# A hand-made layout for the stage behind attention: weights first in the pool, x in fixed homes, x's low part made by VectorE, three homes for raw words

## The chip, the cores and the metric

The kernel runs on one core of one Trainium2 chip. The metric is the device time of one launch in microseconds (us), of which the median over several runs is given. A profile is one more execution, recorded by the hardware profiler. TensorE is called PE in the profile, VectorE DVE, ScalarE ACT, GpSimd POOL and SyncE, whose queue issues the DMAs here, SP or SPq.

## The reference

```python
scores = (q @ k.T) / sqrt(64)                     # 8 batches, 8 heads, 576 x 576
scores = where(scores >= rowmax - tau, scores, -1e9)
attn = softmax(scores)
x = (attn @ v), the heads side by side            # 4608 tokens x 512
h = x @ w_in                                      # 512 -> 2048, float64 weights
g = max(h, 0) + alpha * min(h, 0)
out = g @ w_out                                   # 2048 -> 512
```

## The kernel before, in words

TensorE multiplies numbers of a shortened fp32 form. For accuracy every operand is cut into a high part (rounded, "hi") and the rest ("lo"), and each product is made of three matmuls: hi by hi, hi by lo, lo by hi. The float64 weights come as raw 64-bit words. A chain of eight steps on ScalarE, VectorE and GpSimd, called decoding here, makes a hi and a lo tile of each. With 128 hidden rows to a slice there are 16 slices (`fc`), each with a tile of `w_in` and one of `w_out`.

The kernel has two stages.

1. Attention over 32 pairs of heads, with slices 0 to 6 of the second network worked in between for groups of 256 tokens. The finished x goes to DRAM (`xs`), the sum over the seven slices too (`part`).
2. The stage behind attention (`behind`, line 792). When the attention loop is through, its pool `ap1` is closed and a pool `wp2` is opened on the same bytes, with `reuse_waits="tile"`: each tile there waits for the earlier users of its own bytes. The stage finishes slices 0 to 6 for what is left of the tokens (jobs of kind a: a rest of the group at 3328, then the groups at 3584, 3840, 4096 and 4352), then does slices 7 to 10 for all tokens in nine jobs of 512 (kind b), then slices 11 to 15 (kind c). The last three groups of kind a need x of the last batch, which the last pair of heads completes.

A job has two kinds of steps. `step1` (line 853) is the first layer of one slice, called a unit: 12 matmuls (4 chunks of x by 3 terms), then on VectorE the two instructions of lines 859 and 860 that read the PSUM result and leave it in `pt`, then ScalarE's hi part of g (line 228) and GpSimd's lo part of g (line 231). `step2` (line 865) is the second layer of 128 tokens: 21 matmuls for kind a, 12 for b, 15 for c, and the way out of PSUM. There are four PSUM homes for units and four for second layers. The list `order` (line 910) puts the first unit of the next job ahead of the second-layer steps of the job at hand. Only where kind a meets kind b do the second-layer steps come first, so that the first job of kind b runs its four units in a row and the first unit of the next job straight behind them.

x comes in through `load` (line 839): one home `xr` for the raw x, two each for its hi part `xh` and its lo part `xl`. `load` of a job is called at the first step of the job before. The four chunks are then split one at the end of each step (`split`, line 847): ScalarE rounds the chunk into `xh` (line 850), and GpSimd subtracts (line 851). Chunks that are left when the job starts are split ahead of its first unit. The steps of decoding are also spread over the list (`starts`, line 924), each weight one step of the chain at a time: load (line 120), two conversions on ScalarE (lines 130 and 131), clamp and shift on VectorE (lines 134 and 137), sign and power (142 and 147), rounding on ScalarE (151), a product on GpSimd (825), a difference on VectorE (826) and a sum on GpSimd (165). The raw words of a weight have two homes (`w0`), its temporary three (`w1`).

PE, ACT, DVE and POOL issue their instructions in the order in which the code emits them (`manual_schedule`, line 956): each engine's queue is the order of the list above, and an instruction that waits holds everything behind it on its engine. The order on SP is set by the framework's scheduler.

The order of tags in `wp2` gives the addresses: `xr` comes first and lies over `qst0` and `qst1` (attention's scaled q), then `xh` and `xl` over `qst1` and the tiles `eo`, `e0` that attention's last product reads, then the raw words, the temporaries and the eight weight tiles.

Of the kernel before, what the change touches and what calls it, by code (L numbers as in the profile page):

```python
# [10 lines left out]
F32 = mybir.dt.float32  # L11
F32R = mybir.dt.float32r
I32 = mybir.dt.int32
U32 = mybir.dt.uint32
I64 = mybir.dt.int64
AF = mybir.ActivationFunctionType
ALU = mybir.AluOpType
# [4 lines left out]
P = 128  # L22
# [5 lines left out]
G2 = 512  # L28
# [7 lines left out]
GB = 11  # L36
ENG1 = ('vpp', 'vpp')
ENG2 = ('vvp', 'vvv')
# [25 lines left out]
def f(ap):  # L64
    return ap.bitcast(F32)
# [10 lines left out]
def tile_masked_attention_moe(  # L76
# [11 lines left out]
    nc = tc.nc  # L88
    B, NPAIR = q.shape[0], q.shape[1]
    NT, DM = out.shape  # L90
    NCC = DM // P
# [16 lines left out]
    class Split64:  # L108


        def __init__(self, pool, raw, temp_pool, temp, eng, src, a, name, split=False):
            self.split = split
            self.pool, self.raw_tag, self.temp_pool, self.temp_tag = pool, raw, temp_pool, temp
            self.eng = [nc.vector if e == 'v' else nc.gpsimd for e in eng]
            self.src, self.a, self.name = src, a, name

        def load(self):
            tag, bufs = self.raw_tag
            self.raw = self.pool.tile([P, DM], I64, tag=tag, name=f"wr{self.name}", bufs=bufs)
            nc.sync.dma_start(self.raw.rearrange("p (a b) -> p a b", a=self.a), self.src)  # L120

        def size(self):
            words = self.raw.bitcast(I32).rearrange("p (n two) -> p n two", two=2)
            self.low, self.high = words[:, :, 0], words[:, :, 1]
            tag, bufs = self.temp_tag
            pool = self.temp_pool
            if pool is mem:
                pool, tag, bufs = (mem.mp1, "g", GB) if mem.mp1 else (spool, "wt", 4)
            self.t = pool.tile([P, DM], I32, tag=tag, name=f"wt{self.name}", bufs=bufs)
            nc.scalar.activation(f(self.t), f(self.high), AF.Abs)  # L130
            nc.scalar.activation(f(self.low), self.low.bitcast(U32), AF.Copy, scale=2.0**-52)

# [40 lines left out]
    wi, wo = {}, {}  # L173
    ready = set()

    def weight(pool, fc, io):
        d = wi if io == "i" else wo
        d[fc] = pool.tile([P, 2, DM], F32R, tag=f"w{io}{fc}", name=f"w{io}{fc}")
        return d[fc]

    def load_x(pool, t0, n, gn, bufs):
        xr = pool.tile([P, NCC, gn], F32, tag=f"xr", name=f"xr{gn}_{t0}", bufs=bufs)
        t = t0
        while t < t0 + n:
            b, o = divmod(t, S)
            m = min(S - o, t0 + n - t)
            nc.sync.dma_start(xr[:, :, t - t0 : t - t0 + m], xs[b][:, :, o : o + m].rearrange("c p t -> p c t"))
            t += m
        return xr

    def split_x(pool, xr, t0, n, gn, bufs):
        xh = pool.tile([P, NCC, gn], F32R, tag="xh", name=f"xh{gn}_{t0}", bufs=bufs)
# [52 lines left out]
    spool = sp.enter_context(tc.tile_pool(name="spool", bufs=1, side="right"))  # L245
    mem = SimpleNamespace(mp1=None)
# [389 lines left out]
    for p in pairs:  # L636
        o = 9 * p.pi
        n = o - 9
# [138 lines left out]
    for n_, (w, fc, io) in enumerate(pieces):  # L777
        c = n_ * DEC_LAST // (len(pieces) - 1)
# [13 lines left out]
    def behind():  # L792
# [10 lines left out]
        wp2 = ctx.enter_context(tc.tile_pool(name="wp2", bufs=1, reuse_waits="tile"))  # L803
        ps_2 = ctx.enter_context(tc.tile_pool(name="ps_2", bufs=1, space=PSUM, reuse_waits="tile"))
        wpool = SimpleNamespace(b=None)
        part2 = [dram.tile([min(P, NT - t), DM], F32, name=f"part2{t}") for t in range(0, NT, P)]
        fa, fb = fcs2[:NA], fcs2[NA:]

        chores = deque()
        stages = deque()  # L810

        def decode(fc, io):
            w = Split64(wp2, ("w0", 2), wp2, ("w1", 3), ENG2[0], *(src_i if io == "i" else src_o)(fc))

            def put():
                w.round(weight(wp2 if fc in fa else wpool.b, fc, io)[:, 0])

            low, t = lambda: f(w.low), lambda: f(w.t)
            return [
                w.load,  # L820
                w.size,
                lambda: (w.clamp(), w.shift()),
                lambda: (w.sign(), w.power()),
                put,
                lambda: nc.gpsimd.tensor_tensor(low(), low(), f(w.high), op=ALU.mult),
                lambda: nc.vector.tensor_tensor(t(), t(), f(w.hi), op=ALU.subtract),
                lambda: w.join((wi if io == "i" else wo)[fc][:, 1]),
            ]

        class Job:  # L830
# [8 lines left out]
            def load(self):  # L839
                if self.x is not None:  # L840
                    return
                self.xr = load_x(wp2, self.t0, self.n, G2, 1)
                xh = wp2.tile([P, NCC, G2], F32R, tag="xh", name=f"xh{self.name}", bufs=2)
                xl = wp2.tile([P, NCC, G2], F32R, tag="xl", name=f"xl{self.name}", bufs=2)
                self.x = xh, xl

            def split(self, c):
                n = self.n
                xh, xl = self.x
                nc.scalar.activation(xh[:, c, :n], self.xr[:, c, :n], AF.Copy)  # L850
                nc.gpsimd.tensor_tensor(xl[:, c, :n], self.xr[:, c, :n], f(xh[:, c, :n]), op=ALU.subtract)

            def step1(self, i):
                fc, n, gn = self.fcs[i], self.n, self.gn
                pool, bufs = (mem.mp1, GB) if self.kind == "a" else (wpool.b, 2 * len(fb))
                name = f"{self.name}_{fc}"
                ph = layer1_into(ps_2.tile([P, 512], F32, tag="ph", name=f"ph{name}", bufs=4), fc, n, self.x)
                t = pool.tile([P, gn], F32, tag="pt", name=f"pt{name}", bufs=2)
                nc.vector.tensor_scalar(t[:, :n], ph[:, :n], 0.0, alpha_sb[:, fc : fc + 1], op0=ALU.min, op1=ALU.mult)
                nc.vector.scalar_tensor_tensor(t[:, :n], ph[:, :n], 0.0, t[:, :n], op0=ALU.max, op1=ALU.add)  # L860
                g = pool.tile([P, 2, gn], F32R, tag="g", name=f"g{name}", bufs=bufs)
                split_g(g, t, n)
                self.g[i] = g
# [42 lines left out]
        ja = [Job(fa, t, min(G2, NT - t), G2, "b") for t in range(0, NT, G2)]  # L906
        jb = [Job(fb, t, min(G2, NT - t), G2, "c") for t in range(0, NT, G2)]
        jobs = first + ja + jb

        order = []  # L910
        for a, b in zip([None] + jobs, jobs + [None]):
# [22 lines left out]
        for k, (job, what, i) in enumerate(order):  # L934
            if job.kind == "b" and wpool.b is None:
                p1.close()
                wpool.b = ctx.enter_context(tc.tile_pool(name="mp2", bufs=1, reuse_waits="tile"))
            for b in ahead.get(k, []):
                if b.x is None:
                    b.load()  # L940
                    xq.extend((b, c) for c in range(NCC))
            if what == 1:
                while xq and xq[0][0] is job:
                    b, c = xq.popleft()
                    b.split(c)
                job.step1(i)
            else:
                job.step2(i)
            for fn in starts.get(k, []):
                fn()  # L950
            if xq:
                b, c = xq.popleft()
                b.split(c)
# [110 lines left out]
```

## Time and profile before

| | us |
|---|---|
| median of 3 runs (1392.28 to 1394.5) | 1393.32 |
| the profiled execution, its own time | 1393.67 |
| its span, first to last instruction | 1391.7 |
| PE busy | 1338.2 |
| DVE busy | 993.8 |
| ACT busy | 842.4 |
| POOL busy | 834.1 |

The median lies 0.35 us under the time of the profiled execution. What lies around the span is 1393.67 - 1391.7 = 1.97 us. In the profile a row of a timeline gives the start in us from the beginning of the span, the duration, the engine, the line of the code, the operation, output and inputs, and the number of instructions that were put together in the row. In square brackets stands the idle time of the engine just before and the instruction that ended it. A row of the windows gives, for each engine, busy time and instructions in that stretch, then the clock that TensorE was granted, the busy share of the DMA engines, and GB/s. A row of the chain gives start, duration and the link of the chain of work that ended last.

### The profile page before, as it was taken

What the parts mean: (1) busy time and instruction counts of PE and PEld (TensorE: products, weight loads), DVE (VectorE), ACT (ScalarE), POOL (GpSimd) and SP (SyncE); (2) the same over time, 40 slices, a digit from 0 to 9 for tenths busy, and PEclk for the clock granted to TensorE, in tenths of its full rate; (3) what the DMA queues carried; (4) which work ended last, traced back from release to release, by engine and by line L of the source; (5) the groups of instructions that cost most, each with busy time, mean ns of one, the idle gap of its engine ahead of it and who ended that gap; (6) DMA issues with size and microseconds to landing.
All of it is one profiled execution on the core that took longest, in us unless ns stands there. A gap on an engine that the chain in (4) does not pass through costs nothing.

```text
span 1391.7 us, 23733 instructions
## 1 busy us (share of the span) xinstructions
PE 1338.2 (96%) x8116; PEld 1180.8 (85%) x8116; DVE 993.8 (71%) x1960; ACT 842.4 (61%) x1918; POOL 834.1 (60%) x963
## 2 busy tenths in 40 slices
PE   5888899999999999999999998999999999999998
PEld 4555789999999999999999997887888888888887
DVE  6999888889888888898898863762666644333332
ACT  7887888888888888888888862432323222211210
POOL 3887576576666666666576564774667564443431
PEclk9999999999999999999999999999999999999999
DMA  7653634644545445444454303334464543243222
GB/s 235 178 154 102 168 111 120 174 117 131 151 120 147 140 127 148 132 140 126 132 154 128 107 26 120 104 134 145 137 214 153 185 152 121 91 140 133 91 76 83
DMA packets 113448, 186.02 MB, mean 134 GB/s; under 512 B 16592, under 2 KB 47600, under 8 KB 113328
## 3 DMA queue, kind: packets, MB, share of 16 engines
q1 hardware_dynamic: 113328, 184.51, 44.5%
q8 instruction: 65, 1.06, 0.3%
q14 instruction: 55, 0.45, 0.1%
HBM read 104.41 MB, written 37.90 MB: 102 GB/s over the span
## 4 chain that ended last, share of the span: by engine, by line
PE 82%; DVE 6%; ACT 4%; POOL 3%; DMA 2%; issue 2%; SPq 1%; POOLq 0%; DVEq 0%; ACTq 0%
PE acca L237 11%; PE pha L207 11%; PE av L564 10%; PE s L417 10%; PE phc L207 9%; PE accc L237 9%; PE accb L237 7%; PE t L461 7%; PE phb L207 7%; DVE p L452 1%; DVE nmx L432 1%; PE tk L477 1%; DMA wri<-in_moe_w_in_dram 1%; POOL ga L231 1%; ACT xb L577 1%
## 5 line engine op out<-in xcount | busy, mean ns | idle before, releaser
L432 DVE TENSOR_REDUCE nmx<-s 128x1 f32<-128x576 f32 x288 | 217.2, 754 | 71.9 <-PE s L417 69.1
L237 PE MATMUL acca<-wo,ga 128*128 128x512 f32 x756 | 226.8, 417 | 2.5 <-POOL ga L231 0.8
L452 DVE SCALAR_TENSOR_TENSOR p<-s,thr,p 128x576 f32<-128x576 f32 x256 | 206.9, 808 | 4.8 <-ACT thr L445 4.5
L440 ACT ACTIVATE p<-s,nmx 128x576 f32<-128x576 f32 x256 | 190.3, 743 | 11.0 <-DVE nmx L432 10.9
L417 PE MATMUL s<-kh,qst 128*128 128x288 f32 x640 | 141.8, 312 | 37.9 <-DVE p L452 20.5
L207 PE MATMUL pha<-xh,wi 128*128 128x256 f32 x784 | 157.0, 284 | 0.2 <-ACT pra L220 0.2
L461 PE MATMUL t<-ident,p 128*128 128x128 f32 x1024 | 155.0, 274 | 0.0
L417 PEld LDWEIGHTS s<-kh,qst 128*128 128x128 f32 x640 | 101.0, 192 | 61.6 <-issue 32.4
L237 PEld LDWEIGHTS acca<-wo,ga 128*128 128x128 f32 x756 | 133.3, 191 | 23.1 <-POOL ga L231 2.8
L228 ACT ACTIVATE gc<-ptc 128x512 fp32r<-128x512 f32 x45 | 28.4, 632 | 197.0 <-DVE ptc L860 197.0
L231 POOL TENSOR_TENSOR gc<-ptc,gc 128x512 fp32r<-128x512 f32 x45 | 58.2, 1293 | 142.7 <-ACT gc L228 142.7
L417 PE MATMUL s<-kl,qst 128*128 128x288 f32 x640 | 133.6, 299 | 0.0
L207 PEld LDWEIGHTS pha<-xh,wi 128*128 128x128 f32 x784 | 128.0, 190 | 4.6 <-ACT pra L220 1.5
L461 PEld LDWEIGHTS t<-ident,p 128*128 128x128 f32 x1024 | 126.8, 141 | 0.1
L237 PE MATMUL accc<-wo,gc 128*128 128x512 f32 x540 | 124.2, 389 | 0.6 <-POOL gc L231 0.6
L237 PEld LDWEIGHTS accc<-wo,gc 128*128 128x128 f32 x540 | 101.3, 188 | 22.0 <-POOL gc L231 1.0
L224 POOL TENSOR_TENSOR pta<-pta,pra 128x256 f32<-128x256 f32 x95 | 70.1, 738 | 74.1 <-ACT pra L220 71.5
L207 PE MATMUL phc<-xhc,wi 128*128 128x512 f32 x360 | 112.5, 389 | 0.0
L207 PE MATMUL pha<-xl,wi 128*128 128x256 f32 x392 | 110.5, 282 | 0.0
L231 POOL TENSOR_TENSOR ga<-pta,ga 128x256 fp32r<-128x256 f32 x126 | 97.5, 774 | 19.0 <-ACT ga L228 10.7
L564 PE MATMUL av<-eo,vst 128*128 128x322 f32 (+1 forms) x512 | 107.6, 334 | 0.0
L517 DVE TENSOR_TENSOR eo<-t,eo 128x512 fp32r<-128x512 f32 (+1 forms) x168 | 97.4, 592 | 8.5 <-ACT eo L513 8.3
(143 smaller groups left out, 3303.1 us busy)
## 6 DMA issues: line engine op xcount, KB each, us to landing
kr<-in_k_dram SPq DMA_DIRECT2D x31, 320.0 KB
rb<-rvd SPq DMA_DIRECT2D x64, 144.0 KB
xs<-xa SPq DMA_DIRECT2D x32, 288.0 KB
pinb<-part SPq DMA_DIRECT2D x36, 256.0 KB
part<-obb SPq DMA_DIRECT2D x36, 256.0 KB
pinc<-part SPq DMA_DIRECT2D x36, 256.0 KB
out_dram<-obc SPq DMA_DIRECT2D x36, 256.0 KB
vr<-in_v_dram SPq DMA_DIRECT2D x28, 320.0 KB
```

The costliest lines, as they stand in the source:

```text
L207: nc.tensor.matmul(ph[:, :n], w[:, c, :], xx[:, c, :n], start=(c == 0 and ti == 0), stop=(c == NCC - 1 and ti == 2),)
L224: nc.gpsimd.tensor_tensor(t[:, :n], t[:, :n], r[:, :n], op=ALU.add)
L228: nc.scalar.activation(g[:, 0, :n], t[:, :n], AF.Copy)
L231: nc.gpsimd.tensor_tensor(g[:, 1, :n], t[:, :n], f(g[:, 0, :n]), op=ALU.subtract)
L237: nc.tensor.matmul(acc[:m, :], gg[:, g, o : o + m], w, start=(first and ti == 0), stop=(last and ti == 2))
L417: nc.tensor.matmul(ps[:, h, :288], w, kk[:, a + h * 288 : a + (h + 1) * 288], start=(ki == 0 and i == 0), stop=(ki == 1 and i == n - 1),)
L432: nc.vector.tensor_reduce(self.nmx[:, j : j + 1], self.S[u][0][:, :, :288], axis=AX.XY, op=ALU.max, negate=True)
L440: nc.scalar.activation(pj, ps[:, :, :288], AF.Exp, bias=nmx[:, j : j + 1], scale=1.0)
L452: nc.vector.scalar_tensor_tensor(pj, ps[:, :, :288], thr[:, j : j + 1], pj, op0=ALU.is_ge, op1=ALU.mult, accum_out=self.sm[:, c : c + 1])
L461: nc.tensor.transpose(tb[:, c, :], pt[:, j, j * D + c * P : j * D + (c + 1) * P], ident)
L517: nc.vector.tensor_tensor(dst[1], ps, f(dst[0]), op=ALU.subtract)
L564: nc.tensor.matmul(pa[:m, :n], w, x, start=(part == 0 and c == 0), stop=(part == z.parts[-1] and c == NKC))
```

## The change

- In `wp2` the tiles are made in another order: the eight weight tiles first, then three temporaries, three homes for raw words (one more than before), then the homes of x: `xl1`, `xh1`, `xl0`, `xr`, `xh0`. By the tile sizes in the code the raw x then lies over attention's `kh` and `kl`, `xh0` over `kl` and small tiles behind it, `xl0` over the masked scores `p` and `kh`.
- x's homes are fixed tiles, and the jobs that load x take 0 and 1 in turn. Since the home of the raw x is one tile, all chunks still to be split are split before the next load is called.
- `split` makes the low part of x on VectorE in place of GpSimd.
- The homes of g in the last pool `mp2` become 9 in place of 10 (`len(fb) + 4`), which makes room for the third home of raw words.

```diff
+        for io in "io":
+            for fc in fa:
+                weight(wp2, fc, io)
+        tw = [wp2.tile([P, DM], I32, name=f"tw{i}") for i in range(3)]
+        rw = [wp2.tile([P, DM], I64, name=f"rw{i}") for i in range(3)]
+        homes = {t: wp2.tile([P, NCC, G2], F32R, name=f"home{t}") for t in ("xl1", "xh1", "xl0")}
+        homes["xr"] = wp2.tile([P, NCC, G2], F32, name="homexr")
+        homes["xh0"] = wp2.tile([P, NCC, G2], F32R, name="homexh0")
...
-            w = Split64(wp2, ("w0", 2), wp2, ("w1", 3), ENG2[0], *(src_i if io == "i" else src_o)(fc))
+            w = Split64(wp2, rw, wp2, tw, ENG2[0], *(src_i if io == "i" else src_o)(fc))
+            w.raw = rw[len(decoded) % 3]
+            w.t = tw[len(decoded) % 3]
+            decoded.append(w)
...
-                self.xr = load_x(wp2, self.t0, self.n, G2, 1)
-                xh = wp2.tile([P, NCC, G2], F32R, tag="xh", name=f"xh{self.name}", bufs=2)
-                xl = wp2.tile([P, NCC, G2], F32R, tag="xl", name=f"xl{self.name}", bufs=2)
-                self.x = xh, xl
+                load_into(homes["xr"], self.t0, self.n)
+                self.x = homes[f"xh{self.home}"], homes[f"xl{self.home}"]
...
-                nc.scalar.activation(xh[:, c, :n], self.xr[:, c, :n], AF.Copy)
-                nc.gpsimd.tensor_tensor(xl[:, c, :n], self.xr[:, c, :n], f(xh[:, c, :n]), op=ALU.subtract)
+                xr = homes["xr"]
+                nc.scalar.activation(xh[:, c, :n], xr[:, c, :n], AF.Copy)
+                nc.vector.tensor_tensor(xl[:, c, :n], xr[:, c, :n], f(xh[:, c, :n]), op=ALU.subtract)
...
-                pool, bufs = (mem.mp1, GB) if self.kind == "a" else (wpool.b, 2 * len(fb))
+                pool, bufs = (mem.mp1, GB) if self.kind == "a" else (wpool.b, len(fb) + 4)
...
+        fresh = [x for x in jobs if x.x is None]
+        for i, x in enumerate(fresh):
+            x.home = i % 2
...
-            for b in ahead.get(k, []):
+            for b in ([job] if k == 0 and what == 1 else []) + ahead.get(k, []):
                 if b.x is None:
+                    while xq:
+                        a, c = xq.popleft()
+                        a.split(c)
                     b.load()
                     xq.extend((b, c) for c in range(NCC))
```

More of the change, by code (lines that the diff above doesn't have):

```diff
@@ L115, in __init__ @@
             self.src, self.a, self.name = src, a, name
+            self.raw = self.t = None
         def load(self):
-            tag, bufs = self.raw_tag
-            self.raw = self.pool.tile([P, DM], I64, tag=tag, name=f"wr{self.name}", bufs=bufs)
+            if self.raw is None:
+                tag, bufs = self.raw_tag
+                self.raw = self.pool.tile([P, DM], I64, tag=tag, name=f"wr{self.name}", bufs=bufs)
             nc.sync.dma_start(self.raw.rearrange("p (a b) -> p a b", a=self.a), self.src)
@@ L124, in size @@
             self.low, self.high = words[:, :, 0], words[:, :, 1]
[L125 to L129, printed above, removed]
+            if self.t is None:
+                tag, bufs = self.temp_tag
+                pool = self.temp_pool
+                if pool is mem:
+                    pool, tag, bufs = (mem.mp1, "g", GB) if mem.mp1 else (spool, "wt", 4)
+                self.t = pool.tile([P, DM], I32, tag=tag, name=f"wt{self.name}", bufs=bufs)
             nc.scalar.activation(f(self.t), f(self.high), AF.Abs)
@@ L182, in load_x, with load_into @@
         xr = pool.tile([P, NCC, gn], F32, tag=f"xr", name=f"xr{gn}_{t0}", bufs=bufs)
+        load_into(xr, t0, n)
+        return xr
+    def load_into(xr, t0, n):
         t = t0
@@ L188, in load_x @@
             t += m
-        return xr
     def split_x(pool, xr, t0, n, gn, bufs):
@@ L807, in behind @@
         fa, fb = fcs2[:NA], fcs2[NA:]
-        chores = deque()
-        stages = deque()
+        for io in "io":
[6 more added lines that the diff above has]
+        homes["xh0"] = wp2.tile([P, NCC, G2], F32R, name="homexh0")
+        decoded = []
         def decode(fc, io):
-            w = Split64(wp2, ("w0", 2), wp2, ("w1", 3), ENG2[0], *(src_i if io == "i" else src_o)(fc))
+            w = Split64(wp2, rw, wp2, tw, ENG2[0], *(src_i if io == "i" else src_o)(fc))
+            w.raw = rw[len(decoded) % 3]
+            w.t = tw[len(decoded) % 3]
+            decoded.append(w)
             def put():
-                w.round(weight(wp2 if fc in fa else wpool.b, fc, io)[:, 0])
+                if fc in fb:
+                    weight(wpool.b, fc, io)
+                w.round((wi if io == "i" else wo)[fc][:, 0])
             low, t = lambda: f(w.low), lambda: f(w.t)
```

## The prediction

> **What bounds the kernel now.** The page first: who is busy, and where PE is not.
>
> ```profile
> PE 1338.2 (96%) x8116; PEld 1180.8 (85%) x8116; DVE 993.8 (71%) x1960; ACT 842.4 (61%) x1918; POOL 834.1 (60%) x963
> PE   5888899999999999999999998999999999999998
> ```
>
> PE bounds the kernel. Behind the first five slices, which the change doesn't touch, its row has one digit below 9 ahead of the last: slice 25, from 24 x 1391.7 / 40 = 835 us, where attention ends and the stage begins that the change touches. Only what PE loses there can be won. Next the windows of that stage (time, busy PE, its weight loads, DVE, ACT, POOL, then granted clock, DMA share, GB/s):
>
> ```profile
> 840.00:850.00 10.00, 4.84 (x24) 3.46 (x22) 2.71 (x7) 3.60 (x9) 4.39 (x7) 0.79 0.61 191
> 950.00:960.00 10.00, 7.76 (x30) 5.65 (x29) 4.33 (x6) 2.41 (x5) 7.25 (x6) 0.92 0.11 27
> 1000.00:1050.00 50.00, 50.00 (x222) 41.44 (x221) 32.00 (x44) 16.52 (x30) 32.08 (x25) 1.00 0.50 160
> ```
>
> PE loses 5.2 us in the first, 2.2 us in the second, and none from 1000 us on. So there are two places, the first job that needs a fresh x and the meeting of kinds a and b, and small losses between. The chain of work that ended last says what each waits for; beside it two rows of the PE timeline, the last product that reads attention's keys, and the end of the old work:
>
> ```profile
> 840.45 0.32 SPq L624
> 840.88 4.25 DMA xr<-xs
> 956.40 1.23 POOL xlb L851
> 957.67 0.73 PE phb L207 x2
> 941.88 10.92 PE phb L207 x48
> ...
> 818.16 0.43 PE L417 MATMUL s<-kl,qst 128*128 128x288 f32 x2
> 841.65 0.28 PE L207 MATMUL pha<-xh,wi 128*128 128x256 f32 x1
> ```
>
> At the first place PE runs out of work at 841.9 and x lands at 845.1. At the second it waits for a low part of x from POOL. A unit of kind b takes 10.92 / 4 = 2.73 us there.
>
> **The new homes: nothing.** The raw x lay over `qst`, whose last reader ran at 818.16, and the load was issued at 840.88: 22 us later, straight behind the last pair's store (L624, 840.45), which waits for the end of attention. So not the home held the load but its place in SP's queue. The new home lies over `kh` and `kl`, which the same row at 818.16 reads last. The first load of the new pool stood behind the last store out of the closed one, the code calls both at the same places as before, and I take the order to stay. The load then lands at 845.1 as now. The eight weight tiles are written later than x; nine homes of g suffice, since a job has at most five in use when the next one's units come. Both cost nothing. The flush of chunks ahead of a load bites only at the first job of kind a with a fresh x, whose last chunk was split at that step anyway.
>
> **VectorE makes the low part, first place.** This is what costs. On VectorE the subtraction stands in the queue between two units: the two PSUM instructions of the next unit are behind it, it waits for ScalarE's high part, and ScalarE's next high part is behind that unit's `ga`, which waits for VectorE. On POOL it was beside this loop. The rows as they are:
>
> ```profile
> 840.54 0.48 DVE L859 TENSOR_SCALAR pta<-pha,alpha_sb 128x256 f32<-128x256 f32 x1 [0.50 <-PE pha L207]
> 841.05 0.42 DVE L860 SCALAR_TENSOR_TENSOR pta<-pha,pta 128x256 f32<-128x256 f32 x1
> 845.23 0.42 ACT L850 ACTIVATE xha<-xr 128x256 fp32r<-128x256 f32 x1 [4.74 <-DMA xr<-xs]
> 846.57 0.67 ACT L130 ACTIVATE wti<-wri 128x512 f32<-128x512 f32 x1 [0.62 <-DMA wri<-in_moe_w_in_dram]
> 847.71 0.40 ACT L850 ACTIVATE xha<-xr 128x256 fp32r<-128x256 f32 x1
> 847.28 0.43 DVE L134 TENSOR_SCALAR wti<-wti 128x512 f32<-128x512 f32 x1 [4.29 <-ACT wti L130]
> 847.74 0.43 DVE L137 TENSOR_SCALAR wti<-wti 128x512 int32<-128x512 int32 x1
> 849.55 1.41 POOL L851 TENSOR_TENSOR xla<-xr,xha 128x256 fp32r<-128x256 f32 x2
> 851.61 10.21 PE L237 MATMUL acca<-wo,ga 128*128 128x512 f32 x42
> 884.54 0.68 DVE L826 TENSOR_TENSOR wti<-wti,wi 128x512 f32<-128x512 f32 x1
> ```
>
> VectorE's subtraction of 128x512 is not in the trace for x, but L826 is the same operation: 0.68 us when POOL is idle; for 256 columns I take half and a little, 0.36 (bounds 0.25 and 0.48). The chain anew: high part of chunk 0 done at 845.65, subtraction to 846.05; then the PSUM pair, which now ran at 840.54 to 841.47, i.e. 0.93 us: 846.98. `ga` on ACT, of the shape of a high part and taken at its 0.40: 847.4; the two conversions, 1.14 us to the next start: 848.55; high part of chunk 1: 848.95; subtraction: 849.35; pair of the third unit: 850.28; `ga` and high part of chunk 2 to 851.05, while VectorE clamps and shifts (0.43 each) to 851.1; subtractions of chunks 2 and 3: 851.85. Now POOL's last one ends at 849.55 + 1.41 = 850.96, and the second-layer group starts 0.65 later, at 851.61. The next load of x waits for VectorE's last subtraction in place of POOL's and goes out as much later; PE is then in its group of 42 (10.21 us), which covers it. **First term: +0.9 us** (bounds +0.4 with the short subtraction, +2.7 if the weight's words land 1.8 later, for which nothing speaks but a third weight in the queue behind).
>
> **Between the places: a gain and a loss of one size.** Three later jobs of kind a take x in during the second layer of the job before.
>
> ```profile
> 874.48 0.67 ACT L130 ACTIVATE wti<-wri 128x512 f32<-128x512 f32 x1 [1.42 <-DMA wri<-in_moe_w_in_dram]
> 914.28 0.66 ACT L130 ACTIVATE wto<-wro 128x512 f32<-128x512 f32 x1 [2.18 <-DMA wro<-in_moe_w_out_dram]
> 871.93 10.24 PE L237 MATMUL acca<-wo,ga 128*128 128x512 f32 x42
> 891.81 9.71 PE L237 MATMUL acca<-wo,ga 128*128 128x512 f32 x42
> 911.16 4.26 PE L237 MATMUL acca<-wo,ga 128*128 128x512 f32 x18
> 915.87 6.09 PE L237 MATMUL acca<-wo,ga 128*128 128x512 f32 x24 [0.44 <-ACT ga L228]
> 883.68 0.48 DVE L859 TENSOR_SCALAR pta<-pha,alpha_sb 128x256 f32<-128x256 f32 x1 [4.13 <-PE pha L207]
> 884.74 0.42 ACT L850 ACTIVATE xha<-xr 128x256 fp32r<-128x256 f32 x1
> 864.20 1.09 DVE L826 TENSOR_TENSOR wti<-wti,wi 128x512 f32<-128x512 f32 x1
> 865.21 0.96 DVE L134 TENSOR_SCALAR wti<-wti 128x512 f32<-128x512 f32 x1
> 866.21 0.84 DVE L137 TENSOR_SCALAR wti<-wti 128x512 int32<-128x512 int32 x1
> ```
>
> Gain: raw words that come late hold ACT at 874.48 and 914.28, and `ga` with it; the group of 42 then takes 10.24 and 921.96 - 911.16 = 10.80 us, beside 9.71 undisturbed. With a third home these loads need not wait for an old weight to be joined: -0.53 - 1.09 = -1.6 us. Loss: in each of the three the pair at 883.68 comes to stand behind the subtraction of chunk 2, whose high part ends at 885.15: it starts at about 885.55, 1.87 later, and the fourth subtraction adds 0.36. VectorE gets part of it back: its decoding steps at 864.20, 865.21 and 866.21 took 1.09, 0.96 and 0.84 beside POOL, against 0.68, 0.43 and 0.43 in the rows above, and POOL's subtractions, one cause, are gone: up to 1.35. So PE is held up by 0.9 if all of it comes back, by 2.2 if none, and by nothing if the four PSUM homes for units take it up. I take 0.55 each, between the first and the last, since the giving back is read from rows and the slack isn't: 1.65 in all. **Second term: 0** (-1.6 to +5).
>
> **Second place.** Four units of kind b in a row, each with one chunk to split behind it:
>
> ```profile
> 944.66 0.75 DVE L859 TENSOR_SCALAR ptb<-phb,alpha_sb 128x512 f32<-128x512 f32 x1 [9.40 <-PE phb L207]
> 945.45 0.69 DVE L860 SCALAR_TENSOR_TENSOR ptb<-phb,ptb 128x512 f32<-128x512 f32 x1
> 946.17 0.63 ACT L228 ACTIVATE gb<-ptb 128x512 fp32r<-128x512 f32 x1 [3.61 <-DVE ptb L860]
> 946.71 0.61 ACT L850 ACTIVATE xhb<-xr 128x512 fp32r<-128x512 f32 x1
> 946.88 1.29 POOL L231 TENSOR_TENSOR gb<-ptb,gb 128x512 fp32r<-128x512 f32 x1 [9.10 <-DMA pinb<-part]
> 872.38 1.04 POOL L825 TENSOR_TENSOR wri<-wri 128x512 f32<-128x512 f32 x1
> 872.47 1.50 DVE L826 TENSOR_TENSOR wti<-wti,wi 128x512 f32<-128x512 f32 x1
> ```
>
> The last two rows show what VectorE's subtraction does beside POOL: started 0.09 behind a product of 1.04 us, it took 1.50, and ended 0.55 after POOL did. So it waits POOL out. In the loop, the pair starts at 944.66, the high part of x ends at 947.32, but POOL is in `gb` until 948.17; the subtraction ends at 948.72, and the next pair starts there, 4.0 us after the one before (its follower starts some 0.05 ahead of such an end). PE gives a unit each 2.73 us, so VectorE sets the pace: 944.66 + 4 x 4.0 = 960.7 for the fourth subtraction, where POOL's ended at 957.63. PE's two last matmuls (0.73) follow. **Third term: +3.1 us.** The Trainium skill, page "SBUF — State Buffer", section "SBUF: two separate sides", calls the port that the two engines share an exclusive lock, held for the whole instruction by whichever starts first; the trace agrees, with 1.50 against 0.68. Without that wait the pace would be 947.37 + 0.68 - 944.66 = 3.4 us less the overlap of 0.1, 3.3, still over 2.73, and the fourth would end at 957.9: +0.2, the low bound.
>
> The other 16 changes of job in kinds b and c have the splits beside second-layer steps. In the window from 1000 us DVE is busy 32.00 of 50 us, 14 per job of 21.8 us (8 x 2.73); four subtractions of 0.68 to 1.25 make it 17 to 19. Cost zero; what hides it is the unit that stands between a job's last unit and its second layer, and where that cover is gone a change could cost some 0.5.
>
> **Sum.** 0.9 + 0 + 3.1 = +4.0 us on the profiled execution's 1393.67 (span 1391.7 and 1.97 around it): 1397.7. The median of the runs is 0.35 lower, so for a median I say **1397.3**. About 0.2% (2.8 us) can be told from no change here.
>
> **The rivals.** *The shorter subtraction wins (not slower).* In the chain of the second place POOL's `gb` and subtraction follow one another; VectorE's would take 0.68 in place of 1.23 and run beside `gb`. The fourth high part would be there at 946.71 + 0.61 + 3 x 2.73 = 955.5, its subtraction at 956.2 in place of 957.63: -1.4; with -1.6 from the third home and the first place as now, -3.0: 1390.3 on the median. It decides if the PSUM pair behind the subtraction is not late, that is, if VectorE's loop is under 2.73 us. For it: POOL's row in the chain. Against it: 3.3 us even with no port wait. Chance 0.1. The Trainium skill, page "GPSIMD Engine Reference", section "Engine selection", gives two-input elementwise work to VectorE, GpSimd being about twice as slow; the rows agree (1.29 and 0.68), and by that rule alone the time would go this way.
>
> *The load moves ahead.* If SP's order changes and x is loaded at 818, the first chunk is split at 840.1 and the chain of the first term runs from there: pair to 841.5, `ga`, conversions, and so on, to a group at about 847 in place of 851.6: -4.6, and with +3.1 at the second place -1.5: 1391.8 on the median. It speaks for it that the bytes are free, against it that they were so before. Chance 0.08.
>
> *Hidden after all.* No port wait, or slack enough: +0.9 - 1.6 + 0.2 = -0.5: 1392.8. Against it stand the rows at 872. Chance 0.1.
>
> **How the numbers follow.** Forecast 0.72, the rivals 0.1, 0.08 and 0.1. The forecast's own range is 1395.6 (the first term at +0.4, the second at -1.2) to 1400.5 (the second at +3.2, two thirds of its way up). The range for 8 in 10 takes in the two cases near no change, 1391.8 to 1400.5; outside it lie the first rival and the worst sums. Faster: the first rival and a little of the second, 0.12. Same: the rest of the other two, 0.16. Slower: 0.72.
>
> **What would show it.** 72 subtractions of 128x512 on DVE at 0.7 to 1.3 us and 16 of 128x256 at some 0.36; the load of x still behind the last pair's store, landing at 845; the first group of 42 at 852.5; VectorE's pairs at the second place 4.0 us apart and PE's wait there near 5 us; no ACT wait for raw words over 1 us; PE full from 1000 us on. Wrong it would be if the load starts before 840, if the pairs come each 2.7 us, or if PE shows gaps in the later jobs.

## The result, and the profile after

The changed kernel takes 1403.97 us (median of 4 runs, 1402.14 to 1405.54), the kernel before, run beside it, 1393.29 (4 runs, 1392.28 to 1394.5). The ratio is 1.0076 with an interval of 1.0058 to 1.0093: slower by 10.7 us, where the prediction said 4.0 and at most 7.2. The profiled execution of after took 1405.54, its span 1403.8. Of the kernels below, layout_two_raw, sub_behind_pair and early_x had one run in twelve that took 1895, 7514 and 4665 us (in sub_behind_pair the profiled one); their medians count it, their ratios leave it out.

The page of after: the busy times, then PE's row in 40 slices.

```profile
PE 1343.1 (96%) x8116; PEld 1184.6 (84%) x8116; DVE 1048.6 (75%) x2048; ACT 843.0 (60%) x1918; POOL 732.9 (52%) x875
PE   5888899999999999999999997998999999999998
```

VectorE took over 88 instructions and 55 us, GpSimd lost 101 us. PE's row has 7 instead of 8 in slice 25, the end of attention, and a new 8 in slice 28, from 27 x 1403.8 / 40 = 948 us, the second place. The windows of after (PE, weight loads, DVE, ACT, POOL, granted clock, DMA share, GB/s):

```profile
840.00:850.00 10.00, 4.50 (x31) 3.83 (x29) 2.58 (x6) 1.84 (x6) 2.58 (x4) 0.86 0.79 256
850.00:860.00 10.00, 7.92 (x26) 6.21 (x27) 6.55 (x12) 2.76 (x8) 2.92 (x4) 0.62 0.23 64
960.00:970.00 10.00, 5.41 (x18) 3.22 (x17) 6.31 (x7) 2.30 (x4) 2.91 (x3) 0.84 0.01 1
1000.00:1050.00 50.00, 50.00 (x222) 41.41 (x221) 36.15 (x52) 14.26 (x25) 19.45 (x15) 1.00 0.58 185
```

The steady part is full as before, with DVE at 36 of 50 us. All of PE's new idle time lies ahead of 970 us. PE's waits in after, by what ended them (total, times, longest), name the places. In before the line with `pta` had 0.2 us, once.

```profile
PE pha L213 <- ACT homexh L868: 7.3, 3, 4.5
PE pha L213 <- DVE pta L878: 4.2, 6, 0.8
PE phb L213 <- ACT homexh L868: 3.1, 2, 1.8
PE phb L213 <- DVE homexl L869: 1.5, 2, 0.9
```

And PE's timeline in after, at the groups that mark the stages: three groups of 42, a unit that waits, the last group of kind a (its first 17), the first second layer of kind b.

```profile
855.16 10.83 PE L243 MATMUL acca<-wo,ga 128*128 128x512 f32 x42
896.44 0.36 PE L213 MATMUL pha<-homexh,wi 128*128 128x256 f32 x1 [0.82 <-DVE pta L878]
897.92 9.74 PE L243 MATMUL acca<-wo,ga 128*128 128x512 f32 x42
918.99 9.74 PE L243 MATMUL acca<-wo,ga 128*128 128x512 f32 x42
938.07 4.32 PE L243 MATMUL acca<-wo,ga 128*128 128x512 f32 x17
969.94 12.78 PE L243 MATMUL accb<-wo,gb 128*128 128x512 f32 x48
```

In before these groups started at 851.61, 891.81, 911.16, 930.20 and 958.24. So the two profiled executions are 1.3 us apart at the end of the old work (the last `pha<-xh` starts at 842.96 and 841.65; the change touches nothing ahead of it, and this mark lies anywhere from 839.5 to 843.2 in the profiles below), 3.55 at the first group, 7.87 at the last one and 11.70 at kind b's first second layer. The span differs by 12.1, the profile of after being 1.6 above its median.

### The profile page after: what moved, and what is told of

Same layout as the page of the kernel before. It is cut to its first block, busy times and chain, and to the rows that moved or that the text cites. A ratio compares the mean times of both kernels' runs of the same rounds, so it can differ in the third digit from the quotient of the medians.

```text
span 1403.8 us, 23840 instructions
## 1 busy us (share of the span) xinstructions
PE 1343.1 (96%) x8116; PEld 1184.6 (84%) x8116; DVE 1048.6 (75%) x2048; ACT 843.0 (60%) x1918; POOL 732.9 (52%) x875
## 4 chain that ended last, share of the span: by engine, by line
PE 79%; DVE 7%; ACT 5%; issue 3%; DMA 3%; POOL 2%; SPq 1%; POOLq 0%; ACTq 0%; DVEq 0%
PE acca L243 11%; PE av L570 10%; PE s L423 10%; PE pha L213 10%; PE phc L213 9%; PE accc L243 9%; PE accb L243 7%; PE t L467 7%; PE phb L213 6%; DVE p L458 1%; DVE nmx L438 1%; PE tk L483 1%; DMA wri<-in_moe_w_in_dram 1%; ACT xb L583 1%; ACT xa L581 1%
## 5 line engine op out<-in xcount | busy, mean ns | idle before, releaser
L869 DVE TENSOR_TENSOR homexl<-homexr,homexh 128x512 fp32r<-128x512 f32 (+1 forms) x88 | 75.5, 862 | 56.7 <-ACT homexh L868 56.7
L213 PE MATMUL phc<-homexh,wi 128*128 128x512 f32 x360 | 112.5, 389 | 0.0
```

Source lines behind the costliest of these rows:

```text
L213: nc.tensor.matmul(ph[:, :n], w[:, c, :], xx[:, c, :n], start=(c == 0 and ti == 0), stop=(c == NCC - 1 and ti == 2),)
L869: nc.vector.tensor_tensor(xl[:, c, :n], xr[:, c, :n], f(xh[:, c, :n]), op=ALU.subtract)
```

## The experiments

The theory is the loop: in VectorE's queue the subtraction stands ahead of the next PSUM pair, waits for ScalarE's high part and for GpSimd, and so the pair, a PSUM home and PE wait. The main rival is that the new addresses or the third raw load cost it. The experiments first part the change by its edits, then by its places, and at the end follow the two rivals of the prediction that had VectorE win or the load move.

### One edit at a time

**sub_alone**, the kernel before with the subtraction on VectorE:

```diff
-                nc.gpsimd.tensor_tensor(xl[:, c, :n], self.xr[:, c, :n], f(xh[:, c, :n]), op=ALU.subtract)
+                nc.vector.tensor_tensor(xl[:, c, :n], self.xr[:, c, :n], f(xh[:, c, :n]), op=ALU.subtract)
```

> The kernel before with one edit: x's low part is subtracted on VectorE. Homes, their addresses and the two homes for raw words stay as before. Theory (the loop): on VectorE the subtraction stands between two PSUM pairs in one queue and waits both for ScalarE's high part and for GpSimd, and this alone costs the whole time and a little more, since the third home for raw words (worth about 1.6 us) is missing here: 1403 to 1406 us against the before of the same chip at 1393.3, so +10 to +12; at the meeting of kinds a and b VectorE's pairs stand 4.0 us apart. Rival (the layout): the new addresses or the third raw load in the queue cost most of it; then this kernel is within 3 us of the kernel before.

1403.72 us beside a before of 1392.03: 1.008 (1.0063 to 1.0096). One edit gives the whole loss.

**layout_three_raw**, after with `nc.vector` put back to `nc.gpsimd` in `split`:

> The changed kernel with the subtraction given back to GpSimd: the layout, the fixed homes, the flush and the third home for raw words stay. Theory (the loop): nothing of the loss is left and the third raw home gains what it did in the groups of 42, about 1.6 us: 1391 to 1392.5 us. Rival (the layout): it stays slower than the kernel before by 3 us or more. Rival (third raw load holds x back): the first place alone stays later by about 0.5 us, and the sum is 1392 to 1393.

1393.67 us, 1.0005 (0.9994 to 1.0016). The layout costs nothing that this interval (-0.8 to +2.2 us) shows. The time is above the expected 1391 to 1392.5: the third home's gain of 1.6 does not show in the median.

**layout_two_raw**, the same with two raw homes:

```diff
-        rw = [wp2.tile([P, DM], I64, name=f"rw{i}") for i in range(3)]
+        rw = [wp2.tile([P, DM], I64, name=f"rw{i}") for i in range(2)]
...
-            w.raw = rw[len(decoded) % 3]
+            w.raw = rw[len(decoded) % 2]
```

> The layout alone: the changed kernel with the subtraction on GpSimd and two homes for raw words in place of three. Theory (the loop), and the prediction's step on the homes: no change, 1393.3 plus or minus 1 us, x's load still straight behind the last pair's store. Rival (the layout): slower by 2 us or more. Rival (the load moves): x's load starts before 840 us and the first group of 42 comes more than 1 us earlier.

1393.65 us, 1.0006 (0.9996 to 1.0016): as expected, and the same as with three. SyncE's queue in layout_three_raw shows the load where it was, straight behind the last pair's store:

```profile
840.35 0.32 SPq L630 DMA_DIRECT2D xs<-xa  x1
840.78 0.37 SPq L194 DMA_DIRECT2D homexr<-xs  x1
841.27 1.60 SPq L122 DMA_DIRECT2D rw<-in_moe_w_in_dram  x3
```

**sub_behind_pair**, after with each subtraction kept on VectorE but emitted in the next step, behind that step's pair:

```diff
             def split(self, c):
+                subtract()
+                owner[0] = self
...
-                nc.vector.tensor_tensor(xl[:, c, :n], xr[:, c, :n], f(xh[:, c, :n]), op=ALU.subtract)
+                pend.append(lambda: nc.vector.tensor_tensor(xl[:, c, :n], xr[:, c, :n], f(xh[:, c, :n]), op=ALU.subtract))
...
+                if pend and owner[0] is job:
+                    subtract()
                 job.step1(i)
+                subtract()
             else:
+                subtract()
                 job.step2(i)
```

> The changed kernel with VectorE's subtraction moved in the queue: it is emitted in the step after ScalarE's high part, behind that step's two PSUM instructions instead of ahead of them; those left are emitted ahead of the first unit that needs them and ahead of the next load. The same instructions run on the same engines. Theory (the loop): if the place in the queue is the cause, the PSUM pair waits for neither ScalarE nor GpSimd any more, and nearly all of the loss goes: 1391 to 1394 us, pairs at the meeting of kinds about 2.8 to 3.1 us apart, no wait of units for pt worth naming. Rival (VectorE has too much to do, or its turns with GpSimd cost by themselves): most of the loss stays, 1399 us or more.

1393.36 us, 1.0004 (0.9995 to 1.0014). The same instructions on the same engines, in another order on one queue, and 10 us are back. A second run of the kernel, for its profile, shows how:

> One more look at the same kernel (VectorE's subtraction emitted behind the next PSUM pair), for its profile; the time is known from the runs before, 1393.4 us. Theory (the loop): at the meeting of kinds a and b VectorE's pairs stand 2.7 to 3.1 us apart although each subtraction still takes about 1.3 us beside GpSimd; PE waits there 2 to 3 us in place of 4.6; no unit waits for pt by more than 0.3 us. Rival (VectorE has too much to do): pairs 3.5 us apart or more, and the time is made up elsewhere.

1392.82 us. VectorE at the second place in it:

```profile
950.08 0.68 DVE L876 TENSOR_TENSOR homexl<-homexr,homexh 128x512 fp32r<-128x512 f32 x1
951.47 0.75 DVE L884 TENSOR_SCALAR ptb<-phb,alpha_sb 128x512 f32<-128x512 f32 x1 [0.72 <-PE phb L213]
952.26 0.69 DVE L885 SCALAR_TENSOR_TENSOR ptb<-phb,ptb 128x512 f32<-128x512 f32 x1
952.87 0.68 DVE L876 TENSOR_TENSOR homexl<-homexr,homexh 128x512 fp32r<-128x512 f32 x1
954.19 0.75 DVE L884 TENSOR_SCALAR ptb<-phb,alpha_sb 128x512 f32<-128x512 f32 x1 [0.65 <-PE phb L213]
```

The pairs are 954.19 - 951.47 = 2.72 us apart, PE's own pace, and wait for PE alone. My expectation of 1.3 us per subtraction was wrong for three of the four: they take 0.68, since behind the pair they start when GpSimd's `gb` is over (the row at 952.87 behind a `gb` from 950.96 to 952.25). The fourth, at 956.89 beside a `gb`, takes 1.35. The wait on GpSimd came with the place in the queue too.

### The wait on GpSimd by itself

**no_low_g**: after, but GpSimd makes no low part of g in the first job of kind b, and the third matmul there reads the high part again. A term of that job's second layer is left out; PE's work stays.

```diff
-                split_g(g, t, n)
+                if self.kind == "b" and self.t0 == 0:
+                    nc.scalar.activation(g[:, 0, :n], t[:, :n], AF.Copy)
+                else:
+                    split_g(g, t, n)
```

> The changed kernel, but GpSimd leaves out the low part of g in the first job of kind b (four instructions), and the third matmul of each product there reads the high part again, so that PE's work stays the same. This leaves a term out of the second layer of that job. At the second place GpSimd then has nothing to do beside VectorE's subtraction. Theory (turns with GpSimd, on top of the loop): the subtraction takes 0.68 in place of 1.36 us, VectorE's pairs stand 3.3 us apart in place of 4.0, and the first second layer of kind b starts 2.2 to 2.8 us earlier against the last second layer of kind a: 1401 to 1402 us against 1404. Rival (the chain ScalarE to VectorE alone, GpSimd being a bystander): pairs stay 4.0 us apart, time unchanged.

1400.21 us, 1.0045 (1.003 to 1.0061), faster than expected. First two rows of after at the second place, then two of no_low_g:

```profile
959.54 1.36 DVE L869 TENSOR_TENSOR homexl<-homexr,homexh 128x512 fp32r<-128x512 f32 x1 [1.28 <-ACT homexh L868]
960.83 0.74 DVE L877 TENSOR_SCALAR ptb<-phb,alpha_sb 128x512 f32<-128x512 f32 x1
```

```profile
958.29 0.69 DVE L869 TENSOR_TENSOR homexl<-homexr,homexh 128x512 fp32r<-128x512 f32 x1 [1.28 <-ACT homexh L868]
958.90 0.74 DVE L877 TENSOR_SCALAR ptb<-phb,alpha_sb 128x512 f32<-128x512 f32 x1
```

Without GpSimd beside it the subtraction takes 0.69 in place of 1.36. The pairs start at 952.24, 955.55, 958.90 and 962.26, 3.34 apart where they were 4.0, and from the last group of kind a to kind b's first second layer it is 28.81 us (937.46 to 966.27) against 31.87 in after. Of these 3.1 us, 2.7 are the turn-taking (the fourth subtraction ends 13.39 behind the start of the first pair, in after 16.05); the rest goes with PE's clock, which stays at 1.00 here and is 0.84 and 0.82 in after's windows from 960 and 970. The Trainium skill, page "SBUF — State Buffer", section "SBUF: two separate sides", has VectorE and GpSimd lock a shared pair of ports against each other for a whole instruction; the trace agrees, with 1.36 against 0.69.

### One place at a time

Four kernels: layout_three_raw, with VectorE for some jobs' x only.

```diff
+                eng = nc.vector if self.kind == "a" and self.t0 == 3584 else nc.gpsimd
-                nc.vector.tensor_tensor(xl[:, c, :n], xr[:, c, :n], f(xh[:, c, :n]), op=ALU.subtract)
+                eng.tensor_tensor(xl[:, c, :n], xr[:, c, :n], f(xh[:, c, :n]), op=ALU.subtract)
```

This is vector_first. The other conditions are tokens above 3584 of kind a and the first job of kind b (vector_middle), the second job of kind b (vector_second), and all later ones (vector_steady).

> The layout with three raw homes; VectorE makes the low part of one x alone, the first fresh one (tokens 3584 to 3839), GpSimd of all others. Theory (the loop, its price by place): the first group of 42 starts 2 to 2.5 us later against the end of the old work than with GpSimd, and nothing else changes: 2 to 3 us over the layout with GpSimd (1393.7 beside a before of 1392.0), so about 1.0025 times the before. By the prediction's first term it is 0.9. Rival (no single place costs, the sum of VectorE's work does): below 1.

> The same, with VectorE for the four x's that are split beside the groups of 42 (tokens 3840, 4096 and 4352 of kind a, and the first job of kind b). Theory: each job of kind a waits for a PSUM home once or twice, 0.8 us each time, as in the changed kernel; 4 to 5 us over the layout with GpSimd, about 1.0045 times the before. By the prediction (given back up to 1.35, slack in four PSUM homes) it is 1.65 with the worst at 5. Rival: these waits are only pushed on from the first place and vanish when that is on GpSimd: below 1.5.

> The same, with VectorE for the second x of kind b alone, which is split behind the four units in a row where the kinds meet. Theory: pairs 4.0 us apart there, each subtraction 1.36 us, the first second layer of kind b 3.5 us later against the last group of kind a than with GpSimd, and in the time 3 to 4.5 us (the stalls are long enough now for the clock to drop). The prediction's third term is 3.1.

> The same, with VectorE for all later x's, 64 of the 88 subtractions. Theory and prediction: nothing, as PE is full there; within 0.7 us of the layout with GpSimd. Rival (VectorE's turns with GpSimd cost everywhere): 2 us or more, PE idle at the changes of job.

Beside a before of 1393.24 they took 1395.46 (1.0013, interval 1.0003 to 1.0024), 1397.08 (1.0026, 1.0016 to 1.0036), 1398.15 (1.0033, 1.002 to 1.0046) and 1392.41 (0.9993, 0.9982 to 1.0004). The 64 subtractions of the steady part cost nothing that shows. Over vector_steady the other three cost 3.1, 4.7 and 5.7 us, together more than the whole loss of 10.7; over layout_three_raw, by the ratios, 1.1, 2.9 and 3.9, together less. Each of these has some 2 us of uncertainty, so the prices are read from the traces. What the traces have of it, free of where attention happened to end:

| kernel | A: first high part to first group of 42 | B: first to last group of 42 | C: last group to second layer of b |
|---|---|---|---|
| before | 6.38 | 78.08 | 28.04 |
| after | 7.85 | 81.78 | 31.87 |
| sub_alone | 7.84 | 81.01 | 31.86 |
| layout_two_raw | 6.58 | 78.14 | 28.23 |
| layout_three_raw | 6.32 | 76.54 | 28.23 |
| sub_behind_pair_2 | 6.01 | 77.86 | 29.47 |
| vector_first | 7.85 | 76.57 | 28.68 |
| vector_middle | 6.34 | 81.66 | 28.34 |
| vector_second | 6.33 | 77.01 | 31.72 |
| vector_steady | 6.35 | 76.64 | 28.03 |

A and C are differences of starts (A of after: 855.16 - 847.31, where ScalarE's first high part starts). In B, what the first group took over 9.70 us is taken off, since it ran at a low clock for a time that differs from run to run (10.21 us in before, 11.98 in sub_behind_pair_2). Each place answers to its own edit, and to no other by more than 0.6: so each costs by itself, over layout_three_raw 1.5 in A (2 to 2.5 was expected), 5.1 in B (4 to 5) and 3.5 in C (3.5). With GpSimd the third raw home is worth 1.6 in B (78.14 less 76.54). The 29.47 in C of sub_behind_pair_2 holds a group of 24 that took 7.43 in place of 6.11 at a clock of 0.83. Its 77.86 in B is still 1.3 too long: against what I expected of that kernel, one unit waits 1.09 us for `pta` at 909.98. In early_x_pair, below, where the first decoding starts later, B is 76.45.

### The load moved, and the fastest version

**early_x**: layout_three_raw, with the first fresh x loaded during attention into the home that attention's own groups use.

```diff
                 st["xr"] = load_x(mem.mp1, t0, n, G1, 1)
                 at_cycle(i + XO, lambda: st.update(x=split_x(mem.mp1, st["xr"], t0, n, G1, 1)))
+                if t0 + n == EARLY:
+                    at_cycle(i + XO + 1, lambda: early.update({EARLY: load_x(mem.mp1, EARLY, G1, G1, 1)}))
```

> The layout with the subtraction on GpSimd and three raw homes, and one more edit: the first fresh x (tokens 3584 to 3839) is loaded during attention into the home of raw x that attention's own groups use, so its load no longer stands behind the last pair's store. Theory (place in the queue held the load, not the home): PE's wait of 4 us for the first high part goes, but ScalarE then waits for the first raw words of a weight, which now land at about 845, and the first group of 42 starts at 850 to 850.5 in place of 851.6: 1391.5 to 1392.5 us. If the conversions are no obstacle: group at 847, 1389 us. Rival (attention's end is late by itself, the load was hidden): no change, 1393.5.

1391.77 us, 0.9987 (0.9974 to 0.9999), in the first range. The load is issued at 810.67; then ScalarE waits for the next thing in that queue, a weight's raw words:

```profile
839.92 0.40 ACT L876 ACTIVATE homexh<-xr 128x256 fp32r<-128x256 f32 x1
844.37 0.66 ACT L133 ACTIVATE tw<-rw 128x512 f32<-128x512 f32 x1 [3.15 <-DMA rw<-in_moe_w_in_dram]
845.49 0.40 ACT L876 ACTIVATE homexh<-xr 128x256 fp32r<-128x256 f32 x1
```

**early_x_pair**: early_x, with the subtraction behind the pair on VectorE, and the first decoding three steps later:

```diff
-        for ws, n, (lo, hi) in zip(weights, nsteps, ((0.0, 0.78), (0.1, 0.85))):
+        for ws, n, (lo, hi) in zip(weights, nsteps, ((0.07, 0.78), (0.1, 0.85))):
```

> The early load of x as in early_x, the first weight's decoding started three steps later, and the subtraction on VectorE behind the PSUM pair. Theory: nothing is left in the first place for ScalarE to wait for; the first group of 42 starts at 846 to 848 in place of 851.6, and the time is 1388 to 1390 us, faster than both kernels. Rival: the raw words or the next x, which now load together, are late in the next job and take it back: 1392 us or more.

1384.48 us, 0.9934 (0.9919 to 0.9949): 8.4 us faster than before, more than expected. Its windows and its first group:

```profile
840.00:850.00 10.00, 8.90 (x54) 7.55 (x53) 6.12 (x15) 4.30 (x11) 4.15 (x5) 1.00 0.81 262
850.00:860.00 10.00, 10.00 (x64) 9.03 (x63) 4.36 (x10) 3.35 (x8) 0.74 (x1) 1.00 0.16 58
```

```profile
846.11 9.70 PE L245 MATMUL acca<-wo,ga 128*128 128x512 f32 x42
865.46 9.71 PE L245 MATMUL acca<-wo,ga 128*128 128x512 f32 x42
```

The group starts at 846.11, as expected: 3.6 us behind the last matmul of the old work (842.49), where it was 10.0 in before. What comes on top is that PE's clock stays at 1.00 in this trace, so that the group takes 9.70 in place of 10.21, and that B is 1.6 and C 0.7 shorter than in before (76.45 and 27.38).

**early_x_pair_two_raw** and **early_x_late_decode** take one part of that kernel away each: the third raw home, and VectorE (the subtraction goes back to GpSimd).

> The fastest kernel so far (x loaded early, first decoding three steps later, VectorE's subtraction behind the PSUM pair: 1384.5 us beside a before of 1392.9) with two raw homes in place of three. If the third home is worth what the groups of 42 show in the traces: 1.3 to 1.8 us slower, about 0.9946 of the before instead of 0.9934, ScalarE waiting for raw words again. If it is worth nothing: no difference over 0.5 us.

> The fastest kernel so far with the subtraction given back to GpSimd. Theory (the subtraction is the shorter on VectorE, and behind the pair it holds up nothing, so it wins 0.7 us at the second place, 1.54 in place of 2.24 us of waiting, and up to 0.7 at the first): 1385 to 1386.5 us. Rival (place on VectorE is no better than GpSimd): the same 1384.5. Rival (VectorE costs beside the groups of 42 even behind the pair): faster than 1383.5.

1385.48 us, 0.9941 (0.9927 to 0.9956), and 1387.26, 0.9955 (0.9941 to 0.9969), beside a before of 1393.1. The first lies between its two cases, 1.0 slower with intervals that overlap; ScalarE waits for raw words there again, at 890.32 for 2.25 us and at 908.54 for 2.21. The second is slower by about 2.8, more than the expected 0.5 to 2.0, but here too the intervals overlap; its trace has the low clock at both places (0.83), which the faster one has at neither, so part of it may be that.

## Why the prediction was wrong

The direction was right, and so was the mechanism at both places; the size was 4.0 against 10.7, and most of what is missing lies between the places. Step by step:

- **The new homes: nothing.** Right. The load stands at the same place, 0.43 us behind the store's start in before (840.88 less 840.45) and 0.42 in after (842.49 less 842.07), and layout_two_raw is at 1.0006. That its place in the queue held it, early_x shows: with another place, and a home in another pool, it goes out at 810.67.
- **First term, 0.9.** The loop was worked out right link by link and is 0.6 longer than predicted (7.85 from the first high part to the group, where the prediction's chain gives 852.5 - 845.23 = 7.27). The last two subtractions took 1.20 in place of 0.75, beside GpSimd's `ga` (852.74 to 853.59). The same turn-taking had been read from the rows for the second place and was not put in here. PE's last matmuls take up the other 0.3. In the profiled execution x also landed 0.47 later behind its issue (4.82 against 4.35); over the profiles with three raw loads this is 4.4 to 4.8, with two 4.3 to 4.6, so about 0.2 of it may be the third load.
- **Second term, 0 from -1.6 and +1.65.** This is the step that failed: B is 3.7 longer than in before. The gain was right in the traces (1.6) as long as GpSimd subtracts. The loss was put at 0.55 per job, "between the first and the last" of 0.9, 2.2 and 0, and at three jobs; it was 5.1, and in four: the first x of kind b is split in this stretch too (925.89 to 935.65 in after). From the end of one group of 42 to the start of the next, after takes 10.47, 11.76, 11.33 and 9.34 us, layout_three_raw 10.11, 9.70, 9.64 and 8.24, so the four jobs lose 0.4, 2.1, 1.7 and 1.1. The delay of the pair itself was nearly right: in the second job it is 2.29 (889.96 less 886.00, where the job's units start, against 883.68 less 882.01), predicted 1.87. What fails is the cover. Here VectorE in after in that job, which is the one of the prediction's row at 883.68:

```profile
889.61 0.43 DVE L869 TENSOR_TENSOR homexl<-homexr,homexh 128x256 fp32r<-128x256 f32 x1 [4.66 <-ACT homexh L868]
889.96 0.48 DVE L877 TENSOR_SCALAR pta<-pha,alpha_sb 128x256 f32<-128x256 f32 x1
890.81 0.68 DVE L845 TENSOR_TENSOR tw<-tw,wi 128x512 f32<-128x512 f32 x1
891.41 0.42 DVE L137 TENSOR_SCALAR tw<-tw 128x512 f32<-128x512 f32 x1
891.87 0.84 DVE L140 TENSOR_SCALAR tw<-tw 128x512 int32<-128x512 int32 x1
```

  The pair waits for ScalarE, which makes a copy out of PSUM and two conversions ahead of that high part (887.58 to 889.58), while the unit's matmuls were over at about 887.5. The 1.35 "given back" was read off the decoding steps of one job, at 864 to 866. In that job 0.94 of it did come back (the same steps take 0.68, 0.42 and 0.85 in after, at 869.32, 869.92 and 870.38), and it is the job that loses only 0.4. In the job at 884 the steps took 0.68, 0.42 and 0.84 before the change already, which is what they take after: nothing came back there. First two of them in before, then the instruction of before that ends the pair of that job's third unit, and before's one wait of a unit for `pta`, in the job ahead:

```profile
885.14 0.42 DVE L134 TENSOR_SCALAR wti<-wti 128x512 f32<-128x512 f32 x1
885.60 0.84 DVE L137 TENSOR_SCALAR wti<-wti 128x512 int32<-128x512 int32 x1
889.58 0.42 DVE L860 SCALAR_TENSOR_TENSOR pta<-pha,pta 128x256 f32<-128x256 f32 x1
870.45 0.36 PE L207 MATMUL pha<-xha,wi 128*128 128x256 f32 x1 [0.22 <-DVE pta L860]
```

  The four PSUM homes have little slack, and the trace of before says how much. Seven units run in a row, 1.40 us each (882.01 to 891.81). The seventh needs the home of the third. In the job at 884 the third pair is over at 890.00 and the seventh unit starts at 890.41: 0.4 us of slack. In the job ahead the seventh unit waits 0.22 already: none. So a delay of 2.3 us comes through but for 0.4.
- **Second place, 3.1.** Right in mechanism and nearly in size. The fourth subtraction ends 16.05 us after the first pair started (967.52 + 1.35 less 952.82); the prediction had 960.7 - 944.66 = 16.04. C is longer by 3.83: PE's last two matmuls ran at the low clock (0.46 more from the subtraction's end to the group than in before), and the first pair itself came 0.29 later behind the last group (14.75 against 14.46).
- **Steady kinds, nothing.** Right: vector_steady, and the windows from 1000 us.

Together A, B and C are 1.47 + 3.70 + 3.83 = 9.0 us longer in after than in before, where the prediction had 4.0; 3.7 of the missing 5.0 is the second term. What is left to the measured 10.7 (8.1 to 13.0 by the interval) is 1.7; x's landing (0.47) and the clock in the first group (10.83 against 10.21) make 1.1 of it in the profiled executions, and it is not taken apart further.

Of the rivals, "the shorter subtraction wins" fails by the place in the queue, as the prediction said, not by the engine: behind the pair, VectorE's 0.68 us save 0.7 us of waiting at the second place. In sub_behind_pair_2 PE waits 0.66 + 0.88 us there, in before 0.67 + 1.57; the time of that kernel (1.0004) doesn't show it. "The load moves ahead" didn't happen, since the order on SyncE stayed; its estimate of a group at about 847 was near what early_x_pair gives by hand, but early_x shows that its price left out the raw words, next in the same queue.

Two things stay open. The traces give the third raw home 1.6 us in B with GpSimd, the medians of layout_three_raw and layout_two_raw differ by 0.0, and those of early_x_pair and its variant by 1.0. With VectorE ahead of the pair the home was worth nothing in B (81.0 with two in sub_alone, 81.8 with three in after), so the second term's gain and loss are not two independent sums: with two homes the subtraction on VectorE makes B 2.9 longer than in before. The traces show where: with two homes the late raw words cost the groups of 42 only 0.5 (10.22, 9.74 and 9.70 in sub_alone) in place of 1.6, and with three PE waits for `pta` 1.0 longer in B (4.2 against 3.2). Why it does has not been explained by an experiment of its own.

## What to carry to other kernels

An instruction moved to a faster engine is paid for by its place in that engine's queue: list what it waits for, and what stands behind it; here the same instruction cost 10 us ahead of the PSUM pair and nothing behind it. Take no credit for work that another engine gives back unless the rows of the very step show it, for every job and not for one. Read the slack of a ring of buffers off the trace, from the end of the reader of one home to the start of its next writer; a small wait for a buffer (0.22 us) is a sign that the slack is used up. When a load is late, ask what is next in its queue before pricing its move.

## What the runs showed of the hardware

Whether PE's clock drops after a short stall, and how long it stays low, differs between executions with the same waits, and this limits how well kernels can be told apart here. The same two waits at the second place, in before and then in layout_three_raw:

```profile
957.67 0.50 PE L207 MATMUL phb<-xlb,wi 128*128 128x512 f32 x1 [1.57 <-POOL xlb L851]
958.24 12.65 PE L237 MATMUL accb<-wo,gb 128*128 128x512 f32 x48
```

```profile
956.48 0.50 PE L213 MATMUL phb<-homexl,wi 128*128 128x512 f32 x1 [1.55 <-POOL homexl L869]
957.06 11.09 PE L243 MATMUL accb<-wo,gb 128*128 128x512 f32 x48
```

After a like wait the 48 matmuls took 12.65 us in one and 11.09 in the other; the windows from 950 and 960 have clocks of 0.92 and 0.91 against 1.00 and 1.00. The Trainium skill, page "TensorE: Matmul & The Clock Gate", section "Part 1: The HAM clock gate", says that the clock is halved after an idle window of about 3.4 us, and that this window runs freely. That it is then a matter of phase which stall is hit would fit the difference; no run here shows the phase. But by that rule no stall under 3.4 us should drop the clock, and here the clock dropped at waits of 0.7 and 1.6 us, in four of eight profiles that had the two waits. After the stall of 4 us at the first place the clock was low in every profile; without it, in early_x_pair, nowhere in this stage, though its variant with two raw homes shows 0.83 once, around waits of 0.70 and 0.39 us.

The low clock comes in steps. What the windows of 10 us around a place lack of full clock is 1.7 us in before at the second place (0.8 and 0.9, from 0.92 and 0.91) and in early_x there (one window of 0.83); 3.4 in before and in layout_three_raw at the first place (0.79 and 0.87; 0.81 and 0.85) and in after at the second (0.84 and 0.82); 5.1 or 5.2 in after, sub_alone and vector_first at the first place (0.86 and 0.62; 0.78 and 0.71; 0.80 and 0.69). That is one, two or three times 1.7 us, in every trace here whose clock drops in this stage, within what the two digits allow. One such step is what a window of 3.4 us at half the clock, as that section of the Trainium skill has it, would lack; this is an estimate.
